# Decode attention of two blocks: V's loads ahead of K's, V's product ahead of K's sums, and another map from rows to partitions

## The chip, the core and the metric

The kernel runs on one core of one Trainium2 chip. The metric is the time of one execution in microseconds (us), as the device measures it. Engines are named as in the profile: PE (matrix engine), DVE (vector engine), ACT (scalar engine), POOL, and SP, which here only issues transfers. The 16 load engines that move data between the chip's main memory and the on-chip memory are called DMA.

## The reference, cut to what matters

Two independent attention blocks A and B, one new token per sequence, each with its own weights and its own cache. The results of the two blocks are put side by side.

```python
# per block: B = 2 sequences, 32 heads, Sk = 8192 tokens, Dh = 192, D = 640, all bfloat16
q = (x @ wq).reshape(B, 1, 32, 192).transpose(0, 2, 1, 3)
scores = einsum("bhqd,bhkd->bhqk", q, k_cache) * 192 ** -0.5
p = softmax(scores)
o = einsum("bhqk,bhkd->bhqd", p, v_cache)
out = o.transpose(0, 2, 1, 3).reshape(B, 1, 32 * 192) @ wo
```

Each K and each V is read once: 2 blocks x 2 sequences x 32 heads x 8192 x 192 x 2 bytes x 2 is 805 MB, nearly all of the 837 MB that are read.

## The kernel before, in words

**Units and thirds.** The work is cut into 16 units of eight heads of one sequence (`UH = 8`, `NU = 16`). A unit's K is 8 x 8192 x 192 numbers; each of the 128 partitions holds a sixteenth of one head, 512 tokens. In before partition p holds head p div 16 and sixteenth p mod 16. K and V of a unit come in three thirds (`NCH = 3`), each a load of 128 rows of `ROW` = 32768 numbers (64 KiB). A third is 170 whole tokens and a fragment. Only three buffers for thirds (`NBUF = 3`) fit on chip; they are taken in turn by the list `loads` (L229 to L233), and SP issues load i when the work that reads load i-3 is done (`done`, L490, and L499 to L501): for a third of K its last sum on PE, `("sl", u, c)`, for a third of V its last product, `("pv", u, c)`.

**K's side.** For a third of K, DVE multiplies the tokens by the unit's q in place, in five pieces (`dve_mul`, names `("m", c, k)`, L303; the fragments go into `pad`, L301). PE sums the 192 products of a token down to 16 with twelve matmuls against the identity (`pe_sum`, `("s", c, k)`, L415) into one of three banks, and DVE reduces these to one score (`dve_red`, `("r", c, k)`, L311). The ten tokens that are left of each third, and the fragments, go through `pe_rest` (`("sl", c)`, L427) and `dve_rest` (`("rl",)`, L315).

**Softmax.** When all scores of a unit are there: the maximum of each partition (`mx`, L319), set out by head with `mask` (`mp`, L322), the maximum over partitions on POOL (`ar`, L339), its negative for each partition (`nm`, `nb`), the exponential on ACT (`exp`, L361), and the spread (`sp`, L334), which writes P into `pb`, eight columns a token of which only the partition's head's is not zero.

**V's side.** PE multiplies P by a third of V, two tokens at a time (`pe_pv`, `("pv", c)`, L445 and L451), after `pe_l` (`("l",)`, L433) has summed the exponentials. When the last third is done DVE takes the reciprocal and the two halves of the result (`rc`, `oh`, `os`, L342 to L348), ACT scales it (`of`, L351), and PE puts the eight rows in place in the result of all heads (`pl`, L457).

**The order.** Each engine has one list of instructions, written out by the loop L564 to L608 with `put(engine, unit, name, function, waits)`. In an engine the order of the `put` calls is the order of execution; between engines it is the semaphores of the named waits. In slot u stands K's work of unit u and V's work of unit u-1 (`lag` -1). In before PE's slot u is: sums of K's first third, `l`, V's first third; sums of K's second third, V's second third; sums of K's last third, q of the next unit, V's last third; `pl`. DVE's slot u is: for each third the five products with the reduction of the piece before behind each, and the last reduction; then `rl`, `mx`, `mp`, `nm`, `nb`; `rc`, `oh`, `os`; `sp`. Slots 1 to 15 are emitted as a loop.

**Other places.** The map from rows to partitions stands in the source of the load (`ld_kv`, L269), in `mask` (which partition has which head, L530), and in `esel`, which spreads q from its projection to the partitions (L523, `dve_su` L293, `pe_q` L403). After the last unit, the result is turned (L466) and multiplied by the output weights (L479), which take the buffers of V's first two thirds.

Of the kernel before, what the change touches and what calls it, by code (L numbers as in the profile page):

```python
# [5 lines left out]
ALU = mybir.AluOpType  # L6
ACTF = mybir.ActivationFunctionType
AXL = mybir.AxisListType
# [111 lines left out]
def build_kernel(nc, blocks, out):  # L120
    NBLK = len(blocks)
    B, Hn, Sk, Dh = blocks[0]["k"].shape
# [33 lines left out]
    with ExitStack() as es:  # L156
# [72 lines left out]
        loads = [("k", 0, c) for c in range(NCH)]  # L229
        for u in range(1, NU):  # L230
            for c in range(NCH):
                loads += [("k", u, c), ("v", u - 1, c)]
        loads += [("v", LASTU, c) for c in range(NCH)]  # L233
        buf = {}
        for i, key in enumerate(loads):
# [16 lines left out]
        def dma(out_ap, in_ap, k):  # L252
            s = reg[k][0]
            return lambda eng: eng.dma_start(out_ap, in_ap).then_inc(s, 16)
# [13 lines left out]

        def ld_kv(kind, u, c):  # L269
            qb, hg = u // HG, u % HG  # L270
            src = blocks[qb // B][kind][qb % B, UH * hg:UH * hg + UH].rearrange("h t d -> (h t d)")
            src = src.rearrange("(p n) -> p n", p=128)
            return dma(bufs[buf[kind, u, c]], src[:, c * ROW:(c + 1) * ROW], (kind, u, c))

        def tokens(b, c, lo, n):
            return bufs[b][:, OFF[c] + lo * Dh:OFF[c] + (lo + n) * Dh].rearrange("p (t d) -> p t d", d=Dh)
# [15 lines left out]
        def dve_su(u):  # L292
            return lambda eng: eng.tensor_tensor(su[:], esel[:], onehot[:, S_dve.at(u)].broadcast_to([128, 144]), ALU.mult)  # L293
# [107 lines left out]
            return fn  # L401

        def pe_q(eng):  # L403
            eng.matmul(outps[:, 0:Dh], su[:, 16:144], qc[:, 0:Dh], start=True, stop=False)
            return eng.matmul(outps[:, 0:Dh], su[:, 0:128], qc[:, Dh:QW], start=False, stop=True)  # L405

        def pe_zero(eng):
# [153 lines left out]
        def put(eng, slot, name, fn, waits, lag=0):  # L561
            slots[eng].setdefault(slot, []).append((name, fn, [w for w in waits if w is not None], lag))

        for u in range(NU + 1):  # L564
            real, old = u < NU, u >= 1
            v = u - 1

            def back(*k):
                return k if k[1] >= -1 else None
            if real:  # L570
                put("dve", u, ("su", 1), dve_su(u + 1), [("q", u)])
                for c in range(NCH):
                    for k in range(NSUB):
                        w = [("k", u, c), ("qe", u), ("sl", u - 1, NCH - 1) if u and c == 0 else None]
                        put("dve", u, ("m", c, k), dve_mul(u, c, k), w)
                        put("pe", u, ("s", c, k), pe_sum(u, c, k), [("m", u, c, k), prev(u, c, k)])
                        if k:
                            put("dve", u, ("r", c, k - 1), dve_red(u, c, k - 1),
                                [("s", u, c, k - 1), ("sp", u - 1) if u else None])
                    put("dve", u, ("r", c, NSUB - 1), dve_red(u, c, NSUB - 1), [("s", u, c, NSUB - 1)])  # L580
                    put("pe", u, ("sl", c), pe_rest(u, c),
                        [("m", u, c, NSUB - 1), ("rl", u - 1) if u and c == 0 else None])
                    if c == NCH - 1:
                        put("dve", u, ("rl",), dve_rest, [("sl", u, c)])
                        put("dve", u, ("mx",), dve_max, [("rl", u)])
                        put("dve", u, ("mp",), dve_mp, [("mx", u), ("ar", u - 1) if u else None, ("negm",)])
                        put("dve", u, ("nm",), dve_nm, [("ar", u)])
                        put("dve", u, ("nb",), dve_nb, [("nm", u), ("exp", u - 1) if u else None])
                        put("pe", u, ("q", 1), pe_q, [("su", u + 1), ("qe", u)])
                        put("pool", u, ("ar",), pool_ar, [("mp", u), ("nm", u - 1) if u else None])  # L590
                        put("act", u, ("qe", 1), act_q, [("q", u + 1), ("m", u, NCH - 1, NSUB - 1)])
                    if old:
                        if c == 0:
                            put("pe", u, ("l", -1), pe_l, [("exp", v), ("sp", v), ("os", v - 1), ("rc", v - 1)])
                        put("pe", u, ("pv", c, -1), pe_pv(v, c), [("v", v, c)])
            else:
                put("pe", u, ("l", -1), pe_l, [("exp", v), ("sp", v), ("os", v - 1), ("rc", v - 1)])
                for c in range(NCH):
                    put("pe", u, ("pv", c, -1), pe_pv(v, c), [("v", v, c)])
            if old:  # L600
# [5 lines left out]
            if real:  # L606
                put("act", u, ("exp",), act_exp, [("nb", u), ("l", v) if u else None])
                put("dve", u, ("sp",), dve_spread, [("exp", u), ("pv", v, NCH - 1) if u else None, ("mask",)])  # L608
# [6 lines left out]
        for e, S in streams.items():  # L615
            order = [n for n, *_ in slots[e][1]]
            have = {n for n, *_ in slots[e][0]}
            after = {}
            at = None
            for n in order:  # L620
                if n in have:
                    at = n
                else:
                    after.setdefault(at, []).append(full(n, 0))
            for u in sorted(slots[e]):
                for n, fn, waits, _ in slots[e][u]:
                    S.add(fn, waits=waits, sig=full(n, u), tag=(u, n),
                          pre=after.get(None, ()) if u == 0 and n == order[0] else (),
                          post=after.get(n, ()) if u == 0 else ())

        S_dve.add(dve_oall(0), waits=[("pl", LASTU), ("q", NU)], sig=("oa", 0))
# [84 lines left out]
```

## Time and profile before

| | us |
|---|---|
| median of 3 runs (lowest, highest) | 1956.53 (1955.77, 1956.9) |
| the profiled execution's own time | 1958.03 |
| its span, first to last instruction | 1956.1 |
| PE busy, DVE busy, ACT busy | 1518.4, 1121.2, 28.4 |
| share of the 16 DMA engines, page's part 3 | 99.0% |

The profile is of one execution, and times in its views count from its first instruction. In a timeline each row is: start, duration, engine, line of the code, operation, what it writes and reads, how many (x), and in brackets the engine's idle time just before it and what ended that. In a table by stretches each engine's busy time stands with its number of instructions, then the granted clock of PE, the share of the DMA engines, and GB/s. Busy times of PE are of pipelined instructions, so a start is a better mark than an end.

### The profile page before, as it was taken

The page shows a single profiled execution, that of the slowest core. Times are in us where ns is not written, and L with a number is a line of the kernel's source. Part 1 is how long each engine was busy: PE and PEld are TensorE (multiplying, and loading weights), DVE is VectorE, ACT ScalarE, POOL GpSimd, SP SyncE. Part 2 cuts the span into 40 slices and gives each one's busy share as a digit, 9 for nine tenths or more (in the row PEclk, how much of TensorE's full clock was granted, in tenths as well). Part 3 has the DMA queues.
Part 4 walks back from the last instruction along what each step waited for, and adds up shares of the span by engine and source line. Part 5 has one row for each costly group of instructions (what it writes and reads, how often), then busy time and mean ns, then how long its engine had stood idle before and what let it go on. Part 6 is the DMA issues. An engine that isn't in the chain of part 4 may idle for free.

```text
span 1956.1 us, 18384 instructions
## 1 busy us (share of the span) xinstructions
PE 1518.4 (78%) x8256; PEld 774.8 (40%) x8256; DVE 1121.2 (57%) x771; ACT 28.4 (1%) x76; POOL 8.9 (0%) x60
## 2 busy tenths in 40 slices
PE   4658868688786968968697886868878686886888
PEld 3224434344343433433343443434434343343354
DVE  0686566555665556466546655655566556646610
ACT  0000000000000000000000000000000000000000
POOL 0000000000000000000000000000000000000000
PEclk9789989899898989989899998989989898998999
DMA  9996999999999999999999999999999999999998
GB/s 428 427 425 287 447 429 429 433 429 429 438 434 434 430 430 436 434 436 430 433 433 437 433 430 433 436 434 434 430 433 440 432 430 433 434 437 433 430 433 383
DMA packets 15149, 836.97 MB, mean 428 GB/s; under 512 B 1688, under 2 KB 1824, under 8 KB 2208
## 3 DMA queue, kind: packets, MB, share of 16 engines
q1 hardware_dynamic: 15136, 836.78, 99.0%
q8 instruction: 10, 0.16, 0.0%
q14 instruction: 3, 0.02, 0.0%
HBM read 836.77 MB, written 0.01 MB: 428 GB/s over the span
## 4 chain that ended last, share of the span: by engine, by line
PE 48%; DVE 31%; DMA 13%; issue 7%; ACT 1%; another core or an unknown queue 0%; DVEq 0%; SPq 0%; ACTq 0%; POOL 0%
PE ops L445 30%; DVE big L303 24%; PE scps L415 15%; DMA big<-in_B_k_cache_dram 9%; DVE sc L311 3%; DVE pb L334 2%; PE rest L427 2%; DMA big<-in_B_wo_dram 2%; DMA big<-in_B_wq_dram 2%; PE scps L397 1%; ACT sc L361 1%; PE ops L451 0%; DVE o_hi L345 0%; DVE o_hi L348 0%
## 5 line engine op out<-in xcount | busy, mean ns | idle before, releaser
L415 PE MATMUL scps<-big,ident 128*128 128x512 bf16 x2880 | 737.2, 413 | 374.9 <-DVE big L303 374.6
L303 DVE TENSOR_TENSOR big<-big,qt 128x6144 bf16<-128x6144 bf16 (+1 forms) x240 | 847.8, 3549 | 0.0
L445 PE MATMUL ops<-big,pb 128*40 128x384 bf16 x4080 | 682.0, 327 | 2.4 <-DMA big<-in_B_v_cache_dram 2.4
L415 PEld LDWEIGHTS scps<-big,ident 128*128 128x128 bf16 x2880 | 285.0, 105 | 815.9 <-DVE big L303 455.2
L445 PEld LDWEIGHTS ops<-big,pb 128*40 128x40 bf16 x4080 | 404.5, 100 | 258.1 <-issue 4.3
L311 DVE TENSOR_REDUCE sc<-scps 128x32 f32<-128x512 f32 x240 | 164.6, 686 | 274.1 <-PE scps L415 273.9
L301 DVE TENSOR_TENSOR pad<-big,qt 128x128 bf16<-128x128 bf16 (+1 forms) x64 | 11.8, 205 | 228.1 <-DMA big<-in_B_k_cache_dram 130.2
L342 DVE RECIPROCAL rc<-ops 8x1 f32<-8x1 f32 x16 | 2.5, 156 | 223.8 <-PE ops L445 223.8
L334 DVE TENSOR_TENSOR pb<-sc,mask 128x2048 bf16<-128x2048 f32 x32 | 71.9, 2288 | 19.3 <-ACT sc L361 19.3
L427 PE MATMUL rest<-big,ident 128*128 128x160 bf16 x576 | 48.1, 234 | 0.0
L427 PEld LDWEIGHTS rest<-big,ident 128*128 128x128 bf16 x576 | 43.0, 98 | 11.7 <-issue 0.6
L397 PE MATMUL scps<-big,pb 128*64 128x384 bf16 x160 | 27.7, 336 | 3.2 <-DMA big<-in_B_wq_dram 2.6
L354 ACT ACTIVATE qt<-outps 128x192 bf16<-128x192 f32 x17 | 5.6, 331 | 1579.4 <-PE outps L405 1579.4
L457 PE MATMUL oall<-o_sb,place 8*128 8x192 bf16 x16 | 4.0, 249 | 25.3 <-ACT o_sb L351 25.3
L397 PEld LDWEIGHTS scps<-big,pb 128*64 128x64 bf16 x160 | 18.1, 114 | 12.5 <-DMA big<-in_B_wq_dram 3.0
L293 DVE TENSOR_TENSOR su<-esel,onehot 128x144 bf16<-128x144 bf16 x17 | 5.1, 301 | 28.5 <-PE outps L405 28.5
L389 PE MATMUL rest<-ident,pb 4*128 4x4 bf16 x5 | 0.4, 178 | 21.5 <-DMA pb<-in_B_x_dram 21.5
L315 DVE TENSOR_REDUCE sc<-rest 128x30 f32<-128x480 f32 x16 | 10.5, 658 | 6.9 <-PE rest L427 6.9
L339 POOL PARTITION_ALL_REDUCE mg<-mp x16 | 5.9, 367 | 1855.6 <-DVE mp L322 1855.6
L457 PEld LDWEIGHTS oall<-o_sb,place 8*128 (+1 forms) x16 | 1.4, 90 | 31.4 <-issue 29.5
L290 DVE CAST pb<-rest 128x5 bf16<-128x5 f32 x4 | 0.4, 171 | 19.2 <-PE rest L389 19.2
L361 ACT ACTIVATE sc<-sc,nb 128x512 f32<-128x512 f32 x16 | 11.3, 706 | 2.1 <-DVE nb L328 2.1
(66 smaller groups left out, 131.3 us busy)
## 6 DMA issues: line engine op xcount, KB each, us to landing
big<-in_B_wq_dram SPq DMA_DIRECT2D x1, 7680.0 KB, 37.2
big<-in_A_wo_dram SPq DMA_DIRECT2D x1, 7680.0 KB, 35.0
big<-in_A_wq_dram SPq DMA_DIRECT2D x1, 7168.0 KB, 20.1
big<-in_B_wo_dram SPq DMA_DIRECT2D x1, 4640.0 KB, 32.0
big<-in_B_wo_dram SPq DMA_DIRECT2D x1, 1760.0 KB, 35.8
big<-in_B_wo_dram SPq DMA_DIRECT2D x1, 800.0 KB, 37.3
big<-in_A_wq_dram SPq DMA_DIRECT2D x1, 512.0 KB, 3.6
big<-in_A_k_cache_dram SPq DMA_DIRECT2D x24, 33.7
```

What stands on the lines that cost most here:

```text
L301: eng.tensor_tensor(pad[:, t, lo:hi], src, qt[:, 0, lo:hi], ALU.mult)
L303: return eng.tensor_tensor(t, t, qt[:].broadcast_to([128, size(k), Dh]), ALU.mult)
L311: return lambda eng: eng.tensor_reduce(sc[:, lo:lo + SUB], scps[bank(u, c, k)][:], AXL.X, ALU.add)
L315: eng.tensor_reduce(dst, rest[:, 0:NCH * REST, :].rearrange("p (c t) g -> p c t g", c=NCH), AXL.X, ALU.add)
L334: ins = eng.tensor_tensor(dst[:, :, a], src[:, :, a].unsqueeze(3).broadcast_to([128, TP // 8, 4, UH]), mask[:].unsqueeze(1).unsqueeze(1).b ...
L339: return eng.partition_all_reduce(mg[:], mp[:], 128, bass.bass_isa.ReduceOp.max)
L354: return eng.activation(qt[:, 0, :], outps[:, 0:Dh], ACTF.Identity)
L361: return eng.activation(sc[:], sc[:], ACTF.Exp, bias=nb[:], scale=scale, accum_out=rs[:])
L397: ins = eng.matmul(flat[blk][64 * blk:64 * blk + 64, 0:QW], xz[:, blk, c, XM - m:XM - m + 64], wq_t[blk][:, c, QW * m:QW * m + QW], start= ...
L415: ins = eng.matmul(scps[bank(u, c, k)][:], ident[:], t[:, :, j * DG:(j + 1) * DG], start=(j == 0), stop=(j == NJ - 1))
L427: ins = eng.matmul(rest[:, lo:lo + n, :], ident[:], src[:, :, j * DG:(j + 1) * DG], start=(j == 0), stop=(j == NJ - 1))
L445: ins = eng.matmul(ops[0:MP, 0:QW], pb[:, j0:j0 + MP], bufs[b][:, OFF[c] + j * QW:OFF[c] + (j + 1) * QW], start=(c == 0 and j == 0), stop= ...
```

## The change

The list of loads puts each third of V ahead of the third of K that it was behind. The source of a K or V load is read as 16 sixteenths of 8 heads, so that partition p holds head p mod 8 and sixteenth p div 8; `mask`, `esel` and the column of `pe_q` follow.

On the engines, in slot u from 1 on, V's product of a third now stands ahead of the sums of K's third on PE, `l` ahead of the first. The three DVE steps behind V's last product, and ACT's scaling, stand ahead of the products of K's last third; `pl` stands behind the first sum of that third. The last reduction of a third stands behind the first product of the next third (in unit 0 too). The softmax stands at the end of the slot, and behind it comes the next slot, with V's first product, which reads its P.

```diff
         for u in range(1, NU):
             for c in range(NCH):
-                loads += [("k", u, c), ("v", u - 1, c)]
+                loads += [("v", u - 1, c), ("k", u, c)]
...
         def ld_kv(kind, u, c):
             qb, hg = u // HG, u % HG
-            src = blocks[qb // B][kind][qb % B, UH * hg:UH * hg + UH].rearrange("h t d -> (h t d)")
-            src = src.rearrange("(p n) -> p n", p=128)
-            return dma(bufs[buf[kind, u, c]], src[:, c * ROW:(c + 1) * ROW], (kind, u, c))
+            src = blocks[qb // B][kind][qb % B, UH * hg:UH * hg + UH].rearrange("h t d -> h (t d)")
+            src = src.rearrange("h (i n) -> i h n", n=NCH * ROW)[:, :, c * ROW:(c + 1) * ROW]
+            return dma(bufs[buf[kind, u, c]], src, (kind, u, c))
...
-            eng.matmul(outps[:, 0:Dh], su[:, 16:144], qc[:, 0:Dh], start=True, stop=False)
+            eng.matmul(outps[:, 0:Dh], su[:, 1:129], qc[:, 0:Dh], start=True, stop=False)
...
-        S_dve.add(lambda eng: eng.tensor_copy(esel[:, 16:144].rearrange("p (t y) -> p t y", t=GP)[:, :, 0:16],
-                                              em[:].unsqueeze(2).broadcast_to([128, GP, 16])),
+        S_dve.add(lambda eng: eng.tensor_copy(esel[:, 1:129].rearrange("p (i t e) -> p i t e", t=GP, e=2)[:, :, :, 0],
+                                              em[:].unsqueeze(1).broadcast_to([128, 16, GP])),
...
-        S_dve.add(lambda eng: eng.tensor_reduce(mask[:], ident[:].rearrange("p (h y) -> p h y", y=16), AXL.X, ALU.add),
+        S_dve.add(lambda eng: eng.tensor_reduce(mask[:], ident[:].rearrange("p (i h) -> p h i", h=UH), AXL.X, ALU.add),
...
+            def red(c, k):
+                put("dve", u, ("r", c, k), dve_red(u, c, k), [("s", u, c, k), ("sp", u - 1) if u else None])
+
+            def turn_out():
                 put("dve", u, ("rc", -1), dve_rc, [("pv", v, NCH - 1), ("of", v - 1)])
                 put("dve", u, ("oh", -1), dve_ohi, [("of", v - 1)])
                 put("dve", u, ("os", -1), dve_osum, [("oh", v)])
                 put("act", u, ("of", -1), act_of, [("os", v), ("rc", v), ("pl", v - 1)])
+
+            def v_part(c):
+                if c == 0:
+                    put("pe", u, ("l", -1), pe_l, [("exp", v), ("sp", v), ("os", v - 1), ("rc", v - 1)])
+                put("pe", u, ("pv", c, -1), pe_pv(v, c), [("v", v, c)])
...
+            put("dve", u, ("su", 1), dve_su(u + 1), [("q", u)])
+            for c in range(NCH):
+                if old:
+                    v_part(c)
+                if old and c == NCH - 1:
+                    turn_out()
+                for k in range(NSUB):
+                    w = [("k", u, c), ("qe", u), ("sl", u - 1, NCH - 1) if u and c == 0 else None]
+                    put("dve", u, ("m", c, k), dve_mul(u, c, k), w)
+                    put("pe", u, ("s", c, k), pe_sum(u, c, k), [("m", u, c, k), prev(u, c, k)])
+                    if old and c == NCH - 1 and k == 0:
+                        put("pe", u, ("pl", -1), pe_pl(v), [("of", v)])
+                    if k:
+                        red(c, k - 1)
+                    elif c:
+                        red(c - 1, NSUB - 1)
+                put("pe", u, ("sl", c), pe_rest(u, c),
+                    [("m", u, c, NSUB - 1), ("rl", u - 1) if u and c == 0 else None])
+            c = NCH - 1
+            red(c, NSUB - 1)
+            put("dve", u, ("rl",), dve_rest, [("sl", u, c)])
+            put("dve", u, ("mx",), dve_max, [("rl", u)])
+            put("dve", u, ("mp",), dve_mp, [("mx", u), ("ar", u - 1) if u else None, ("negm",)])
+            put("dve", u, ("nm",), dve_nm, [("ar", u)])
+            put("dve", u, ("nb",), dve_nb, [("nm", u), ("exp", u - 1) if u else None])
+            put("pe", u, ("q", 1), pe_q, [("su", u + 1), ("qe", u)])
+            put("pool", u, ("ar",), pool_ar, [("mp", u), ("nm", u - 1) if u else None])
+            put("act", u, ("qe", 1), act_q, [("q", u + 1), ("m", u, NCH - 1, NSUB - 1)])
+            put("act", u, ("exp",), act_exp, [("nb", u), ("l", v) if u else None])
+            put("dve", u, ("sp",), dve_spread, [("exp", u), ("pv", v, NCH - 1) if u else None, ("mask",)])
```

More of the change, by code (lines that the diff above doesn't have):

```diff
@@ L566, in build_kernel @@
             v = u - 1
[L568 to L599, printed above, removed]
@@ L600, in build_kernel @@
-            if old:
+            def red(c, k):
+                put("dve", u, ("r", c, k), dve_red(u, c, k), [("s", u, c, k), ("sp", u - 1) if u else None])
+            def turn_out():
                 put("dve", u, ("rc", -1), dve_rc, [("pv", v, NCH - 1), ("of", v - 1)])
@@ L604, in build_kernel @@
                 put("act", u, ("of", -1), act_of, [("os", v), ("rc", v), ("pl", v - 1)])
-                put("pe", u, ("pl", -1), pe_pl(v), [("of", v)])
-            if real:
-                put("act", u, ("exp",), act_exp, [("nb", u), ("l", v) if u else None])
-                put("dve", u, ("sp",), dve_spread, [("exp", u), ("pv", v, NCH - 1) if u else None, ("mask",)])
+            def v_part(c):
+                if c == 0:
+                    put("pe", u, ("l", -1), pe_l, [("exp", v), ("sp", v), ("os", v - 1), ("rc", v - 1)])
+                put("pe", u, ("pv", c, -1), pe_pv(v, c), [("v", v, c)])
@@ new lines, in build_kernel @@
+            if not real:
+                for c in range(NCH):
+                    v_part(c)
+                turn_out()
+                put("pe", u, ("pl", -1), pe_pl(v), [("of", v)])
+                continue
+            put("dve", u, ("su", 1), dve_su(u + 1), [("q", u)])
+            for c in range(NCH):
+                if old:
+                    v_part(c)
+                if old and c == NCH - 1:
+                    turn_out()
+                for k in range(NSUB):
[10 more added lines that the diff above has]
+                    [("m", u, c, NSUB - 1), ("rl", u - 1) if u and c == 0 else None])
@@ L627, in build_kernel @@
                     S.add(fn, waits=waits, sig=full(n, u), tag=(u, n),
-                          pre=after.get(None, ()) if u == 0 and n == order[0] else (),
+                          pre=after.get(None, ()) if u == 0 and n == slots[e][0][0][0] else (),
                           post=after.get(n, ()) if u == 0 else ())
```

## The prediction

> **What bounds the kernel now.** I read first the page's slices (share of the load engines and what they moved), then busy time by stretches, then the issues of the loads, then the timeline of TensorE (PE) and VectorE (DVE) over one unit of the steady stretch.
>
> ```profile
> span 1956.1 us, 18384 instructions
> DMA  9996999999999999999999999999999999999998
> GB/s 428 427 425 287 447 429 429 433 429 429 438 434 434 430 430 436 434 436 430 433 433 437 433 430 433 436 434 434 430 433 440 432 430 433 434 437 433 430 433 383
> ```
>
> ```profile
> 60.20:156.90 96.70, 59.95 (x259) 25.25 (x260) 80.49 (x50) 1.15 (x3) 0.37 (x1) 0.83 0.99 423
> 156.90:170.90 14.00, 10.80 (x52) 4.64 (x50) 10.05 (x8) 0.00 (x0) 0.00 (x0) 0.88 0.00 1
> 170.90:1900.00 1729.10, 1372.01 (x7389) 699.63 (x7387) 1024.08 (x676) 22.34 (x60) 5.51 (x15) 0.93 1.00 433
> ```
>
> The load engines are full (share 1.00, last but one column; GB/s in the last) except in one hole of 14.0 us. A load is 128 rows of 64 KiB, 8.389 MB; six of them, one unit (eight heads, their K and V), take 50.33 / 433 = 116.2 us. So loads look like the only bound. The issues say more:
>
> ```profile
> 135.18 0.33 SPq L254 DMA_DIRECT2D big<-in_A_k_cache_dram  x1
> 169.96 0.33 SPq L254 DMA_DIRECT2D big<-in_A_v_cache_dram  x1
> ...
> 866.67 0.33 SPq L254 DMA_DIRECT2D big<-in_A_v_cache_dram  x1
> ...
> 982.73 0.33 SPq L254 DMA_DIRECT2D big<-in_A_v_cache_dram  x1
> 997.03 0.33 SPq L254 DMA_DIRECT2D big<-in_B_k_cache_dram  x1
> ```
>
> The rows at 866.67 and 982.73 are the same issue (the second third of V, released by the first third of K) one unit apart: 116.06 us. Between them the engines' own chain has no slack either:
>
> ```profile
> 880.88 5.35 PE L415 MATMUL scps<-big,ident 128*128 128x512 bf16 x24
> ...
> 896.42 2.76 PE L415 MATMUL scps<-big,ident 128*128 128x512 bf16 x12 [2.10 <-DVE big L303]
> ...
> 899.94 0.34 PE L445 MATMUL ops<-big,pb 128*40 128x384 bf16 x1
> ...
> 914.13 5.45 PE L415 MATMUL scps<-big,ident 128*128 128x512 bf16 x24
> ...
> 929.67 4.42 PE L415 MATMUL scps<-big,ident 128*128 128x512 bf16 x12 [2.10 <-DVE big L303]
> ...
> 935.31 0.34 PE L445 MATMUL ops<-big,pb 128*40 128x384 bf16 x1
> ...
> 959.91 7.24 PE L415 MATMUL scps<-big,ident 128*128 128x512 bf16 x24 [8.52 <-DVE big L303]
> ...
> 982.63 0.19 PE L433 MATMUL ops<-rs,mask 128*8 128x1 f32 x2
> ```
>
> ```profile
> 935.25 0.66 DVE L315 TENSOR_REDUCE sc<-rest 128x30 f32<-128x480 f32 x1 [0.43 <-PE rest L427]
> ...
> 949.60 0.16 DVE L342 RECIPROCAL rc<-ops 8x1 f32<-8x1 f32 x1 [11.75 <-PE ops L445]
> 949.78 0.35 DVE L345 COPY o_hi<-ops 8x192 f32<-8x192 f32 x1
> 950.17 0.34 DVE L348 TENSOR_TENSOR o_hi<-ops,o_hi 8x192 f32<-8x192 f32 x1
> 951.74 4.49 DVE L334 TENSOR_TENSOR pb<-sc,mask 128x2048 bf16<-128x2048 f32 x2 [1.23 <-ACT sc L361]
> ...
> 956.37 0.22 DVE L301 TENSOR_TENSOR pad<-big,qt 128x128 bf16<-128x128 bf16 x1
> ```
>
> PE's work of a third of K (five sums and the rest) and of a third of V follow each other, each starting where the last ended: V 899.94 to 914.13 (14.2), K 914.13 to 935.31 (21.2), V 935.31 to 949.60 (14.3), a break to 959.91 (10.3), K 959.91 to 982.63 (22.7), V 982.63 to 997.03 (14.4), and K once more as from 880.88 to 899.94 (19.1). The sum is 116.2, within rounding of the period: the chain has the loads' pace by its own length, and has no slack to give. A third of K differs by the clock: the last sum takes 2.76 at full clock and 4.42 when it meets a slow stretch. Those come at the same place in each unit, in pieces of about 3.4 us or three of them:
>
> ```profile
> 953.60:963.70 10.10, 3.79 (x9) 1.35 (x10) 9.52 (x6) 0.00 (x0) 0.00 (x0) 0.50 1.00 435
> 977.50:980.80 3.30, 3.30 (x8) 1.14 (x9) 0.49 (x1) 0.00 (x0) 0.00 (x0) 0.50 0.92 397
> 1069.60:1079.70 10.10, 3.73 (x9) 1.35 (x10) 9.58 (x6) 0.00 (x0) 0.00 (x0) 0.50 1.00 435
> 1093.50:1096.90 3.40, 3.40 (x9) 1.20 (x10) 0.54 (x1) 0.00 (x0) 0.00 (x0) 0.50 0.89 386
> ```
>
> The granted clock (third column from the end) is 0.50 throughout these, and full around them.
>
> **The change, part by part.** *The loads' order.* In before the fourth load is the next K, which lies unread while the softmax of unit 0 runs, and V's second third (issued 169.96) waits until that K is summed: that is the hole. With V ahead, V's first third takes the place, and the next free buffer comes from its product with P, which can start right behind the softmax, 14.2 us of PE work, instead of behind a whole third of K. The hole goes: 14.0 us for the loads, worth that much where loads set the end, and nothing where the chain does.
>
> *Unit 0's sums.* The last reduction of a third now stands behind the first product of the next, so DVE no longer waits for it. PE's idle time ahead of the first sum of the second and of the last third goes:
>
> ```profile
> 90.18 6.91 PE L415 MATMUL scps<-big,ident 128*128 128x512 bf16 x24 [3.06 <-DVE big L303]
> ...
> 114.23 6.84 PE L415 MATMUL scps<-big,ident 128*128 128x512 bf16 x24 [3.35 <-DVE big L303]
> ```
>
> That is 6.4 us. Those thirds of K have landed by then, since their products start right behind the reduction.
>
> *The order on PE and DVE from unit 1 on* is the large part, and it is where I part from the loads. Before, a unit's last V product stands behind the last third of K, and covers the row maximum, its spread over partitions and the bias; only from the reciprocal to the first sum is PE idle: 949.60 to 959.91, 10.3 us. After, PE's next work behind the last third of K is the V product of *that* unit's P, which waits for the whole softmax. Its length stands bare in unit 0, from the reduction of the rest to the end of the spread:
>
> ```profile
> 135.18 0.66 DVE L315 TENSOR_REDUCE sc<-rest 128x30 f32<-128x480 f32 x1 [0.43 <-PE rest L427]
> ...
> 138.73 4.49 DVE L334 TENSOR_TENSOR pb<-sc,mask 128x2048 bf16<-128x2048 f32 x2 [0.88 <-ACT sc L361]
> ```
>
> 138.73 + 4.49 - 135.18 = 8.0 us, and 0.15 from there to the first matmul of l (below), where before had 935.31 - 935.25 = 0.1. A second break arises ahead of the last third of K: the reciprocal and the two copies (949.60 to 950.5, 0.9) now stand on DVE ahead of its first product and wait for the last V product, and the product itself is bare, 956.37 to 959.91, 3.5. DVE queues behind that reciprocal all products of the third; PE's sums wait for them. Breaks: 8.1 + 0.9 + 3.5 = 12.5 in place of 10.3, so 2.2 longer. The first products of the other two thirds are covered by V products of 14.2.
>
> Two breaks also mean two slow restarts. Before, one third of K starts after a break (22.7 against 19.1). After, the last third does, and the first V product too. That product after a break is in the tail of before:
>
> ```profile
> 1883.97 0.19 PE L433 MATMUL ops<-rs,mask 128*8 128x1 f32 x2 [4.98 <-DVE pb L334]
> ...
> 1900.56 0.33 SPq L254 DMA_DIRECT2D big<-in_A_wo_dram  x1
> ...
> 1914.63 2.23 SPq L254 DMA_DIRECT2D big<-in_B_wo_dram  x5
> ...
> 1931.32 0.15 DVE L342 RECIPROCAL rc<-ops 8x1 f32<-8x1 f32 x1 [47.50 <-PE ops L445]
> ```
>
> 16.6 from 1883.97 to its end, against 14.2 to 14.4: 2.3 more. So the chain of a unit is 116.1 + 2.2 + 2.3 = 120.6 with one of the two remaining thirds meeting a slow stretch as now, 4.42 - 2.76 = 1.7 less with none, 118.9, and 1.7 more with both, 122.3. Before's stretches keep their place from unit to unit, so the chain settles on a length that brings it back to the same place; among 118.9, 120.6 and 122.3 I take 119.5, one 3.4 us stretch above now. [...]
>
> *The rows.* A load still has the same 128 rows of 64 KiB at the same addresses; only which row goes to which partition changes. At 433 GB/s in every long stretch I take no gain and no loss; the chain now leaves the loads 119.5 - 116.2 = 3.3 us a unit to spare. The set-up of mask, esel and su has as many instructions as before and runs under the first weight loads; weights for q read from an odd column, if slower, lie in the 8 us in which PE idles; uncovered, some tenths a unit.
>
> *The sum.* Unit 0's spread ends at 143.2 - 6.4 = 136.8. Fifteen units of 119.5 bring the last one to 1929.3. From there, by the rows of the tail: 0.15, 16.6, 14.1, 14.3 bring the last reciprocal to 1974.5. From it to the end of the span before took 1956.1 - 1931.3 = 24.8, with waits for the output weights in it:
>
> ```profile
> 1935.65 8.36 PE L479 MATMUL outps<-big,oT 128*2 128x320 bf16 x96 [1.50 <-DMA big<-in_A_wo_dram]
> ...
> 1946.66 5.88 PE L479 MATMUL scps<-big,oT 128*2 128x320 bf16 x80 [0.81 <-DMA big<-in_B_wo_dram]
> ```
>
> After, these are issued some 29 and 15 us ahead of the last reciprocal and land in some 21 and 18 more, just in time; about 2 us go, 22.6 are left: a span of 1997. Against the same row of before (1931.3) that is 43 later. The profiled execution's own time is 1958.03, 1.9 above its span and 1.5 above the median of the runs, 1956.5; so a span of 1997 is a median of 1997.4, and I write 1997.
>
> **The rivals.** *The chain keeps the loads' pace.* If it came out at 116.2 or less, the loads would run full from end to end: by the sum above 1997 - 15 x (119.5 - 116.2) = 1948, and by the loads alone 1956.5 - 14.0 = 1942.5, so 1948. It needs both other thirds at full clock and no slow restart of the V product: 118.9 - 2.3 = 116.6, nearly that. For it: 0.4 is little. Against: every break of 8 us or more on PE in these rows is followed by slow clock. It decides below a chain of 116.8, where 15 x 2.7 = 40.5 less gives the time of before, *no change*.
>
> *The chain settles one stretch higher,* at 122.3 with both thirds slow: 15 x 2.8 = 42 more, 2039. For it: in before two of three thirds of K already meet slow clock. Against: here all three must.
>
> *The loads become slower by the new rows.* It decides from 119.5 / 6 = 19.9 us a load, 421 GB/s. The lowest mean of a long stretch above is 423 (60.2 to 156.9), six loads in 119.0: no effect. The far end is the one load of short rows:
>
> ```profile
> big<-in_A_wq_dram SPq DMA_DIRECT2D x1, 512.0 KB, 3.6
> ```
>
> 0.524 MB in 3.6 us, 146 GB/s, issue and landing included: 345 us a unit and some 5400 in all. The new loads keep their long rows and are nearest to the first, so I price the rival at a tenth under 433: 390, 21.5 us a load, 129 a unit, 1997 + 15 x 9.5 = 2140. [...]
>
> **How the numbers follow.** The forecast gets 0.61, with its own range 1982 to 2015 (chain 118.5 to 120.7); loads' pace at 1948: 0.17; no change by cancellation: 0.03; one stretch higher: 0.11; slower loads: 0.08. The range takes in the first three and the lower part of the fourth: 1942 to 2030. A measurement of this kernel tells 0.2%, 4 us, from no change. Faster is the second case and 0.01 of the forecast's tail, 0.18; same 0.03; slower 0.79.
>
> **What would show it.** The hole near 157 to 171 is gone, and the load engines' share from 250 us on falls from 1.00 to about 116.2 / 119.5 = 0.97, 421 GB/s. The same issue one unit apart is 119.5 us later, not 116.1. PE idles some 8 us ahead of each l, released by DVE's spread, and some 4.4 us ahead of the last third's first sum. I am wrong if DVE still waits for K's landing at the steady pace with the share at 1.00 (first rival), or if single loads take over 19.9 us (last).

## The result, and the profile after

The changed kernel takes 3924.28 us, median of four runs (3908.88 to 3955.93), against 1956.72 us for the kernel before, timed beside it on the same chip (1955.77 to 1957.37, four runs): a ratio of 2.0077, 95% interval 1.9938 to 2.0216. The forecast was 1997, in a range of 1942 to 2030. The profiled execution has a span of 3934.1 us and took 3936.74.

| | before | after |
|---|---|---|
| span of the profiled execution, us | 1956.1 | 3934.1 |
| packets, and MB moved | 15149, 836.97 | 15148, 836.96 |
| share and GB/s in the steady stretch | 1.00, 433 | 1.00, 210 |
| one load of K or V, us | 19.4 | 40.2 |

First the page of the changed kernel: the span, then the share of the load engines and what they moved in 40 slices, then what was moved in all and through which queue.

```profile
span 3934.1 us, 18441 instructions
...
DMA  9999999999999999999999999999999999999998
GB/s 288 213 205 212 208 208 213 211 207 211 211 207 211 213 209 207 213 211 209 209 213 211 207 211 211 208 211 212 210 207 213 208 209 210 209 209 210 207 211 250
DMA packets 15148, 836.96 MB, mean 213 GB/s; under 512 B 1688, under 2 KB 1824, under 8 KB 2208
...
q1 hardware_dynamic: 15136, 836.78, 99.8%
```

The engines are as full as before and have no hole. They move the same bytes in the same number of packets (15136 in the loads' queue, before and after), so no row was cut into pieces; they only move them at half the rate, 210 GB/s against 433. The trace's record of packets says the same row by row: a K or V row of 64 KiB takes 5.07 us in the median and 4.47 at the least, where the kernel before has 2.42 in the median. The first slice, at 288, holds the loads of wq, which the change leaves alone. Next, loads as they were issued in the same kernel: SyncE's (SP's) timeline, in which the second row is six issues behind the first, and then the first load of wq with its median us from issue to landing.

```profile
1021.42 0.54 SPq L254 DMA_DIRECT2D big<-in_A_k_cache_dram  x1
...
1262.88 0.54 SPq L254 DMA_DIRECT2D big<-in_A_k_cache_dram  x1
```

```profile
big<-in_A_wq_dram SPq DMA_DIRECT2D x1, 7168.0 KB, 20.2
```

One unit of six loads takes 241.5 us, 40.2 a load, where 8.389 MB at 433 GB/s take 19.4. The 7.3 MB of wq land in 20.2 us in the same execution, so it is not the chip or the queue that is slow, but these loads. That explains the whole time: there are 96 of them, and the prediction's time by the loads alone, 1942.5, with 96 x (40.2 - 19.4) more is 3939, against 3936.74.

What the engines now wait for, by the view of waits of the changed kernel (us in total, times, longest):

```profile
DVE pad L301 <- DMA big<-in_B_k_cache_dram: 1011.4, 24, 58.9
DVE pad L301 <- DMA big<-in_A_k_cache_dram: 951.2, 24, 58.7
...
PE ops L445 <- DMA big<-in_B_v_cache_dram: 295.8, 24, 27.3
...
PE ops L445 <- DMA big<-in_A_v_cache_dram: 265.6, 24, 15.9
```

VectorE waits for the landing of every one of the 48 thirds of K, 1962.6 us in all, and TensorE for every third of V, 561.4. The kernel before, in the same view:

```profile
DVE pad L301 <- DMA big<-in_B_k_cache_dram: 130.2, 16, 11.6
DVE pad L301 <- DMA big<-in_A_k_cache_dram: 97.9, 14, 10.1
...
PE ops L445 <- DMA big<-in_B_v_cache_dram: 2.4, 1, 2.4
```

There it was 228.1 us for K, and for V next to nothing. The chain of the engines, on which the forecast rested, is now hidden behind the loads altogether.

### The profile page after: what moved, and what is told of

It is laid out like the page before. It is cut to its first block, busy times and chain, and to the rows that moved or that the text cites. A ratio compares the mean times of both kernels' runs of the same rounds, so it can differ in the third digit from the quotient of the medians.

```text
span 3934.1 us, 18441 instructions
## 1 busy us (share of the span) xinstructions
PE 1704.7 (43%) x8256; PEld 828.6 (21%) x8256; DVE 1120.2 (28%) x771; ACT 30.1 (1%) x76; POOL 8.9 (0%) x60
## 2 busy tenths in 40 slices
DMA packets 15148, 836.96 MB, mean 213 GB/s; under 512 B 1688, under 2 KB 1824, under 8 KB 2208
## 3 DMA queue, kind: packets, MB, share of 16 engines
q1 hardware_dynamic: 15136, 836.78, 99.8%
## 4 chain that ended last, share of the span: by engine, by line
another core or an unknown queue 53%; DVE 17%; PE 17%; issue 11%; DMA 1%; POOL 0%; ACT 0%; DVEq 0%; SPq 0%; ACTq 0%; POOLq 0%
DVE big L303 13%; PE scps L415 9%; PE ops L445 7%; DVE sc L311 2%; DMA big<-in_B_wq_dram 1%; DVE pb L334 1%; PE rest L427 1%; PE scps L397 0%; DVE rmax L319 0%; PE outps L479 0%; PE scps L479 0%; POOL mg L339 0%; DVE o_hi L345 0%; DVE o_hi L348 0%
## 5 line engine op out<-in xcount | busy, mean ns | idle before, releaser
L415 PE MATMUL scps<-big,ident 128*128 128x512 bf16 x2880 | 816.6, 446 | 1511.4 <-DVE big L303 1511.4
L445 PE MATMUL ops<-big,pb 128*40 128x384 bf16 x4080 | 779.4, 357 | 561.4 <-DMA big<-in_B_v_cache_dram 295.8
L415 PEld LDWEIGHTS scps<-big,ident 128*128 128x128 bf16 x2880 | 302.5, 111 | 2006.4 <-DVE big L303 1600.3
L445 PEld LDWEIGHTS ops<-big,pb 128*40 128x40 bf16 x4080 | 437.5, 108 | 879.4 <-DMA big<-in_B_v_cache_dram 300.2
L301 DVE TENSOR_TENSOR pad<-big,qt 128x128 bf16<-128x128 bf16 (+1 forms) x64 | 11.9, 207 | 1962.6 <-DMA big<-in_B_k_cache_dram 1011.4
L451 PE MATMUL ops<-big,pb 128*8 128x128 bf16 (+1 forms) x64 | 12.9, 248 | 0.0
## 6 DMA issues: line engine op xcount, KB each, us to landing
big<-in_A_wq_dram SPq DMA_DIRECT2D x1, 7168.0 KB, 20.2
```

The source lines that it names most:

```text
L301: eng.tensor_tensor(pad[:, t, lo:hi], src, qt[:, 0, lo:hi], ALU.mult)
L415: ins = eng.matmul(scps[bank(u, c, k)][:], ident[:], t[:, :, j * DG:(j + 1) * DG], start=(j == 0), stop=(j == NJ - 1))
L445: ins = eng.matmul(ops[0:MP, 0:QW], pb[:, j0:j0 + MP], bufs[b][:, OFF[c] + j * QW:OFF[c] + (j + 1) * QW], start=(c == 0 and j == 0), stop= ...
L451: eng.matmul(ops[0:UH, lo:hi], pb[:, j0:j0 + UH], src, start=False, stop=False, skip_group_check=True)
```

## The experiments

Two questions were open. Is the forecast of the order (a chain of 119.5 us a unit) right where the rows don't hide it? And what makes the new rows slow? For the second there were two theories. **A**: the shape of the source decides, 16 groups of 8 rows in place of 128 even rows, however far apart they lie. **B**: the distance of neighbouring rows decides, 3 MiB in place of 192 KiB. A was later split: **A1**, the shape decides which partitions are written at one time, and the rate goes by those; **A2**, three levels are slow as such. **A3** is that transfers of 64 rows are slow as such. A kernel that a theory holds to be slow was expected at the changed kernel's 40 us a load, some 3900 us in all, and one that it holds to be as fast as before at 19.4 and 1957. For A1 the author assumed that 64 neighbouring partitions from 0 or from 64 on are slow together and that 32 to 95 are not.

The order alone and the rows alone came first. Where one time is given below, the kernel ran once, which is enough to tell 1960 us from 3900.

**The changed kernel with the rows of before.** Order and reductions stay as changed; the partition of each row, mask, esel and the query's weights are those of before.

```diff
-src = blocks[qb // B][kind][qb % B, UH * hg:UH * hg + UH].rearrange("h t d -> h (t d)")
-src = src.rearrange("h (i n) -> i h n", n=NCH * ROW)[:, :, c * ROW:(c + 1) * ROW]
-return dma(bufs[buf[kind, u, c]], src, (kind, u, c))
+src = blocks[qb // B][kind][qb % B, UH * hg:UH * hg + UH].rearrange("h t d -> (h t d)")
+src = src.rearrange("(p n) -> p n", p=128)
+return dma(bufs[buf[kind, u, c]], src[:, c * ROW:(c + 1) * ROW], (kind, u, c))
...
```

> The changed kernel with the rows of before: partition p holds head p div 16 and sixteenth p mod 16, the load's source has two levels again; the order of loads and of the engines stays the changed one. Both theories of the loads (the new source shape, the new distance between neighbouring rows) expect loads of 19.4 us again and a time near 2000. What it tells apart is the order: my chain of 119.5 us a unit gives 1997 with the DMA share at 0.97; the rival, a chain at the loads' pace of 116.1, gives 1942 to 1948 with the share at 1.00.

It took 1995.33 us (1995.10 to 1996.53, four runs), a ratio to before of 1.0203, 95% interval 1.0186 to 1.0220. Busy time by stretches (granted clock, share and GB/s in the last three columns):

```profile
250.00:1900.00 1650.00, 1290.95 (x6806) 652.59 (x6807) 955.10 (x632) 22.05 (x55) 4.75 (x13) 0.93 0.98 422
156.90:170.90 14.00, 9.24 (x36) 3.41 (x34) 11.51 (x6) 0.00 (x0) 0.00 (x0) 0.89 1.04 449
```

SP's timeline of this kernel, the same load one unit apart:

```profile
869.87 0.33 SPq L254 DMA_DIRECT2D big<-in_A_k_cache_dram  x1
...
989.35 0.33 SPq L254 DMA_DIRECT2D big<-in_B_k_cache_dram  x1
```

The hole at 156.9 to 170.9 is gone, the load engines have slack (0.98), and a unit takes 119.48. So the order costs 2%, and what is left of the doubling lies with the rows, which the next kernel has alone.

**The new rows alone**, in the order of before: the reverse edit on the kernel before.

> The kernel before with the new rows alone; the order of loads and engines is that of before. If the rows alone make the loads slow, a load takes 40.1 us as in the changed kernel and the time is 3900 to 3950. If the order has a part in it (V's and K's loads side by side in another sequence), a load is faster than 40 and the time falls clearly under 3900.

It took 3920.16 us. The steady stretch:

```profile
250.00:3800.00 3550.00, 1532.74 (x7330) 744.45 (x7328) 1026.86 (x678) 22.32 (x60) 5.48 (x15) 0.72 1.00 212
```

212 GB/s at a share of 1.00, as in the changed kernel. The rows do it by themselves, and the order makes no difference beside them that these runs could show (3920.16 against 3908.88 to 3955.93).

**The shape with near rows.** Before, with loads of 16 groups of 8 rows where all rows of a group lie 192 KiB apart as before, and the groups nine of those apart.

```diff
+src = blocks[qb // B][kind].rearrange("b h t d -> (b h t d)").rearrange("(r n) -> r n", n=NCH * ROW)
+r = min(128 * (HG * (qb % B) + hg), 1024 - 144)
+src = src[r:r + 144].rearrange("(a b) n -> a b n", b=9)[:, 0:8, c * ROW:(c + 1) * ROW]
+return dma(bufs[buf[kind, u, c]], src, (kind, u, c))
```

> The kernel before, whose loads read other rows: 16 groups of 8 rows, the rows of a group 192 KiB apart as in before, the groups 9 x 192 KiB apart, so that the source can't be folded into two levels (16 is its slowest level). It reads the wrong rows of K and V, as many bytes in rows of the same length, so the output isn't the reference's. [...] Theory B (neighbouring rows 3 MiB apart are slow to read): 19.4 us a load, 1957.

**The distance with the shape of before.** Before, with 128 even rows 1.5 MiB apart.

```diff
+src = blocks[qb // B][kind].rearrange("b h t d -> (b h t d)").rearrange("(p n) -> p n", p=128)
+j = NCH * (HG * (qb % B) + hg) + c
+return dma(bufs[buf[kind, u, c]], src[:, j * ROW:(j + 1) * ROW], (kind, u, c))
```

> The kernel before, whose loads read 128 rows 1.5 MiB apart, a two-level source over all heads of both sequences. It reads the wrong rows of K and V, as many bytes in rows of the same length, so the output isn't the reference's. Theory A (shape of the source): 19.4 us a load, 1957. Theory B (distance of neighbouring rows): clearly slower than 19.4, towards 40, a time of 2300 to 3900.

Near rows in 16 groups took 3930.47 us, and far rows in one level 1958.18. Their steady stretches, in this order:

```profile
250.00:3800.00 3550.00, 1516.26 (x7274) 737.21 (x7271) 1026.88 (x678) 22.32 (x60) 5.48 (x15) 0.72 1.00 211
```

```profile
250.00:1900.00 1650.00, 1305.55 (x6990) 662.73 (x6989) 981.78 (x649) 22.02 (x59) 5.14 (x14) 0.93 1.00 433
```

The distance falls as a cause: eight times before's distance costs nothing, and before's own distance in 16 groups costs everything. Of the two, the shape decides. The next three kernels ask what in it. All three are before with the loads changed.

**A load in two transfers**, partitions 0 to 63 and then 64 to 127, each in two levels:

```diff
-reg[key] = (bsem[i % NBUF], 16 * (i // NBUF + 1))
+reg[key] = (bsem[i % NBUF], 32 * (i // NBUF + 1))
...
+dst = bufs[buf[kind, u, c]]
...
+dma(dst[0:64], src[0:64], (kind, u, c))(eng)
+return dma(dst[64:128], src[64:128], (kind, u, c))(eng)
```

> The kernel before, each K or V load cut in two transfers, partitions 0 to 63 and then 64 to 127; rows, addresses and the two-level source as before. [...] Theory A2 (a source of three levels is slow by itself, whatever partitions the engines write): 19.4 us a load, 1957.

**A load in three transfers**, 32 to 95 first:

```diff
+reg[key] = (bsem[i % NBUF], 48 * (i // NBUF + 1))
...
+for lo, hi in ((32, 96), (0, 32), (96, 128)):
+    ins = dma(dst[lo:hi], src[lo:hi], (kind, u, c))(eng)
```

> The kernel before, each load cut in three transfers, partitions 32 to 95, then 0 to 31, then 96 to 127; rows and addresses as before. [...] Theory A2, or transfers that cost by their number: 19.4 to 20 a load, 1957 to 2010. [...]

**Three levels with the slowest at 128**: each partition gets two pieces of 32 KiB that lie 96 KiB apart.

```diff
+src = src.rearrange("(p x n) -> p x n", p=128, x=2)[:, :, c * (ROW // 2):(c + 1) * (ROW // 2)]
+return dma(bufs[buf[kind, u, c]].rearrange("p (x n) -> p x n", x=2), src, (kind, u, c))
```

> The kernel before with a three-level source whose slowest level is 128: each partition's row is read in two pieces of 32 KiB, 96 KiB apart. It reads other bytes of K and V, as many of them, so the output isn't the reference's. [...] Theory A2 (three levels are slow): 40 us a load, 3900.

The two halves took 3958.64 us, the three transfers 3796.1 and the three levels of 128 took 1963.12. The steady stretch of the halves, the page's slices of the three transfers, and the steady stretch of the three levels:

```profile
250.00:3800.00 3550.00, 1779.38 (x7237) 804.63 (x7236) 1021.66 (x673) 21.16 (x57) 5.48 (x15) 0.62 1.00 208
```

```profile
GB/s 342 249 225 197 205 230 220 235 240 205 190 207 228 238 236 223 221 208 207 228 227 231 233 215 206 210 212 216 211 213 210 211 220 211 211 218 212 210 217 197
```

```profile
250.00:1900.00 1650.00, 1292.73 (x6953) 657.33 (x6952) 981.10 (x649) 21.99 (x59) 5.12 (x14) 0.93 1.00 431
```

A2 falls: three levels run at 431 GB/s, as A1 expected of these. The halves, with two plain levels each, are as slow as 16 groups (208 GB/s against 211). That fits A1 and A3 alike. The three transfers were to tell those apart, and by their time they did not: under A1 I expected about 2885 (9.7 us for half a load at full rate and 19.4 for the other half at half rate, 29 us a load, an estimate from the 19.4 and 40.2 us above), and the time is only 4% under that of the halves. The second slice, the first without loads of wq, stands at 249 GB/s, where the changed kernel has 213, and the later ones swing between 190 and 240 and settle near 211. Their first load tells more. Its 128 rows in two stretches, the 64 rows of partitions 32 to 95 and then the other 64, and a long stretch of the second half beside them:

```profile
38.50:48.20 9.70, 8.74 (x54) 5.99 (x55) 0.00 (x0) 0.00 (x0) 0.00 (x0) 1.00 1.03 434
48.20:67.80 19.60, 4.97 (x31) 2.98 (x29) 0.31 (x1) 0.81 (x2) 0.00 (x0) 0.69 1.00 211
1900.00:3700.00 1800.00, 807.36 (x3827) 391.31 (x3825) 522.72 (x348) 11.90 (x32) 2.92 (x8) 0.73 1.00 215
```

The first load takes 29.3 us, as A1 had it: 64 rows at 434 GB/s (2.42 us a row in the median) and 64 at 211 (5.03). That speaks against A3, since the first of these transfers has 64 rows and is not slow. After that the fast rows die out: in the second half of the run 4 of 6144 rows take less than 2.6 us. The forecast of 2885 took every load to be like the first. So that each rate stands by itself, the next two kernels take the mixture out.

**Only 64 partitions loaded.** Before, where all loads but those of unit 0's K bring only partitions 32 to 95, or only 0 to 63 (in the second kernel).

```diff
+p = slice(0, 128) if kind == "k" and u == 0 else slice(32, 96)
+return dma(bufs[buf[kind, u, c]][p], src[p], (kind, u, c))
```

> The kernel before, whose loads from the first V on bring only the rows of partitions 32 to 95 (half the data; the other half keeps what lies there, so the output isn't the reference's). One transfer of 64 rows a load. [...] Rival A3 (transfers of 64 rows are slow whatever their partitions): 22 us. [...]

> The same with the rows of partitions 0 to 63 alone: as many rows, bytes and transfers as with 32 to 95. [...] Rival A3: the same figure as with 32 to 95, whichever that is. The time is the chain's, 1920 to 1960.

They took 1952.31 and 2050.61 us, a little above the 1920 to 1950 expected for the first and well above the 1920 to 1960 for the second. For a load that finds the queue empty A1 expected 12 us from issue to landing in the first and 22 in the second, estimates from rows of 2.4 and 5 us, and A3 the same in both. Partitions 32 to 95: queue total, median us from issue to landing, and a steady stretch:

```profile
q1 hardware_dynamic: 9184, 446.71, 55.6%
...
big<-in_A_k_cache_dram SPq DMA_DIRECT2D x24, 12.3
```

```profile
1100.00:1900.00 800.00, 638.94 (x3448) 327.19 (x3447) 464.76 (x308) 10.42 (x28) 2.56 (x7) 0.93 0.54 220
```

Partitions 0 to 63, the same three rows:

```profile
q1 hardware_dynamic: 9184, 446.71, 99.3%
...
big<-in_A_k_cache_dram SPq DMA_DIRECT2D x24, 40.2
```

```profile
1100.00:1900.00 800.00, 613.50 (x3210) 308.30 (x3209) 457.44 (x301) 10.09 (x27) 2.19 (x6) 0.91 1.00 206
```

The same number of rows, packets and bytes: the middle 64 partitions need little over half of the time that the engines have (220 GB/s at a share of 0.54, so 407 while they run), and the first 64 need all of it, at 206 GB/s; their 40.2 is mostly waiting in the queue, and 4.194 MB at 206 are 20.4 us a load, against 12.3 from issue to landing. A row takes 2.42 us in the median in the first kernel and 5.12 in the second. Six loads of 20.4 us are 122.4, longer than the engines' 116, which the expected 1920 to 1960 had left out. Both kernels read 64 neighbouring rows at the same distances, so the reading side doesn't tell them apart. A3 falls, and for one transfer of 64 rows A1 holds: **it is which partitions are written together that sets the rate**, 206 GB/s for 0 to 63 and 407 for 32 to 95. Why the two sets differ isn't shown.

**How fine must the groups be?** The shape with near rows again, in 32 groups of 4 rows and in 64 groups of 2. Are these slow like 16 groups of 8, some 3900 us, or as fast as before, 1957?

```diff
-r = min(128 * (HG * (qb % B) + hg), 1024 - 144)
-src = src[r:r + 144].rearrange("(a b) n -> a b n", b=9)[:, 0:8, c * ROW:(c + 1) * ROW]
+r = min(128 * (HG * (qb % B) + hg), 1024 - 160)
+src = src[r:r + 160].rearrange("(a b) n -> a b n", b=5)[:, 0:4, c * ROW:(c + 1) * ROW]
```

```diff
+r = min(128 * (HG * (qb % B) + hg), 1024 - 192)
+src = src[r:r + 192].rearrange("(a b) n -> a b n", b=3)[:, 0:2, c * ROW:(c + 1) * ROW]
```

> The kernel before, whose loads read 32 groups of 4 neighbouring rows, the groups 5 x 192 KiB apart: a three-level source with 32 as its slowest level. It reads wrong rows of K and V, as many bytes, so the output isn't the reference's. [...]

> The same with 64 groups of 2 rows, 3 x 192 KiB apart. [...]

1961.05 and 1956.05 us, with steady stretches:

```profile
250.00:1900.00 1650.00, 1298.08 (x6994) 661.39 (x6992) 981.22 (x649) 22.01 (x59) 5.13 (x14) 0.93 1.00 433
```

```profile
250.00:1900.00 1650.00, 1293.59 (x6988) 659.78 (x6989) 980.87 (x649) 22.00 (x59) 5.12 (x14) 0.94 1.00 433
```

Both run at full rate, 433 GB/s. Of the shapes tried for one transfer to 128 partitions, 16 groups of 8 alone is slow (210 to 212 GB/s), though it writes all 128, the fast 32 to 95 among them. That this shape is slow by the partitions that are written at one time, as A1 has it, was the author's inference from the rates and isn't shown: which engine writes which partition isn't in the records. A cause on the reading side has no run of its own there; the two sources of this shape read groups 192 KiB and 9 x 192 KiB apart, and run alike (210 and 211 GB/s).

**The first third of V ahead, and nothing else.** The last kernel takes from the change only what acts in units 0 and 1: before's rows, before's order from unit 2 on, unit 0's reductions as changed, and one third of V ahead of K in unit 1. Slot 1 is therefore written out, and the loop starts at slot 2.

```diff
-loads += [("k", u, c), ("v", u - 1, c)]
+loads += [("v", 0, 0), ("k", 1, 0)] if (u, c) == (1, 0) else [("k", u, c), ("v", u - 1, c)]
...
+if u == 1 and c == 0:
+    put("pe", u, ("l", -1), pe_l, [("exp", v), ("sp", v), ("os", v - 1), ("rc", v - 1)])
+    put("pe", u, ("pv", c, -1), pe_pv(v, c), [("v", v, c)])
...
+elif c and not u:
+    put("dve", u, ("r", c - 1, NSUB - 1), dve_red(u, c - 1, NSUB - 1), [("s", u, c - 1, NSUB - 1)])
...
```

> The kernel before with two things of the changed order in units 0 and 1 alone: the last reduction of a third behind the first product of the next one in unit 0, and the first third of V ahead of the first third of K in loads and on PE in unit 1. From unit 2 on as before, with before's rows. By my chain theory the unit keeps 116.1, unit 0 is 6.4 shorter and the hole of 14 us in the loads goes: loads full from end to end, 1942, share 1.00. By its rival (a steady chain sets the end, and the hole counts for nothing) 1950, 6.4 less; by the rival that V ahead costs in unit 1 what unit 0 gains: 1955.

It took 1950.09 us (1948.68 to 1951.05, six runs): a ratio to before of 0.9963, 95% interval 0.9949 to 0.9976, so it is faster than before by 0.4%, and the only one of the orders tried that is. By stretches:

```profile
156.90:170.90 14.00, 9.12 (x48) 4.16 (x48) 11.74 (x10) 0.00 (x0) 0.00 (x0) 1.00 1.02 440
170.90:290.00 119.10, 93.25 (x472) 46.31 (x473) 74.81 (x48) 1.49 (x4) 0.37 (x1) 0.89 0.93 397
290.00:1900.00 1610.00, 1273.29 (x6880) 650.11 (x6879) 948.17 (x628) 20.84 (x56) 5.12 (x14) 0.94 1.00 433
```

The hole of 14.0 us is closed, but only 6.2 us come out of it (1956.27, the median of before beside it, less 1950.09), about the 6.4 of unit 0's sums; part of the hole comes back as a share of 0.93 in the next 119 us. This is the rival's 1950, and not the 1942 that I expected for a gain of the whole hole: the engines' chain sets the end, and the loads don't.

## Why the prediction was right or wrong, point by point

**The rows: wrong, and this is the step that failed.** "A load still has the same 128 rows of 64 KiB at the same addresses; only which row goes to which partition changes. At 433 GB/s in every long stretch I take no gain and no loss." The first half is true: bytes and packets are unchanged. The error is to take the rate of 433 GB/s as a property of rows and bytes. It goes with the shape of the load as well (16 groups of 8 rows ran at 210 to 212) and with the partitions written (0 to 63 ran at 206), and the change's new map from rows to partitions brought that shape: 40.2 us a load in place of 19.4. The row of wq that I priced by, 512 KB in 3.6 us, and all loads of before had even rows for their 128 partitions, so no row of before bore on a source of 16 groups. The far end of 5400 was named and then set aside; without a row of that shape the cost was unknown, and a chance of 0.08 was too small for it.

**The rival of slower loads: the right case, at the wrong price.** Its point of decision, 19.9 us a load, was passed by a factor of two. It was priced at 21.5 us a load and 2140 us, "nearest to the first" of two ends because the rows stay long; the time lies between 2140 and the far end of 5400. Distance isn't where the price lay: rows 1.5 MiB apart ran at 433 GB/s, and rows 192 KiB apart in 16 groups at 211. At these distances, with rows of 64 KiB, no run here shows a loss by distance; none has 128 even rows at 2 MiB or 3 MiB.

**The order on PE and DVE: right.** With the rows of before, the forecast of 1997 became 1995.33, and the chain of 119.5 a unit 119.48. Its terms, in the timelines of that kernel (PE, then DVE; start, us, and in brackets the idle time before and its releaser):

```profile
885.42 2.76 PE L415 MATMUL scps<-big,ident 128*128 128x512 bf16 x12 [2.10 <-DVE big L303]
...
918.67 4.45 PE L415 MATMUL scps<-big,ident 128*128 128x512 bf16 x12 [2.10 <-DVE big L303]
...
942.54 4.45 PE L415 MATMUL scps<-big,ident 128*128 128x512 bf16 x12 [4.41 <-DVE big L303]
...
973.41 0.20 PE L433 MATMUL ops<-rs,mask 128*8 128x1 f32 x2 [7.89 <-DVE pb L334]
...
989.25 5.35 PE L415 MATMUL scps<-big,ident 128*128 128x512 bf16 x24
```

```profile
131.10 4.49 DVE L334 TENSOR_TENSOR pb<-sc,mask 128x2048 bf16<-128x2048 f32 x2 [0.88 <-ACT sc L361]
...
938.17 0.16 DVE L342 RECIPROCAL rc<-ops 8x1 f32<-8x1 f32 x1 [18.95 <-PE ops L445]
...
965.38 0.66 DVE L315 TENSOR_REDUCE sc<-rest 128x30 f32<-128x480 f32 x1 [0.43 <-PE rest L427]
...
968.86 4.49 DVE L334 TENSOR_TENSOR pb<-sc,mask 128x2048 bf16<-128x2048 f32 x2 [0.88 <-ACT sc L361]
```

- The bare softmax, 8.0 us: from 965.38 to 968.86 + 4.49 it is 8.0, and PE is idle 7.89 ahead of l. It recurs in every unit, which the waits of this kernel show in one row:

```profile
PE ops L433 <- DVE pb L334: 126.4, 16, 8.0
```

- The break ahead of the last third, 0.9 + 3.5 = 4.4: PE is idle 4.41, and the reciprocal that DVE stands behind is 4.37 ahead of the first sum.
- The second slow restart: the product behind l runs from 973.41 to 989.25, 15.8 where I had 16.6 from the tail. This term was 0.8 too long.
- One of the other two thirds meeting slow clock: of their last sums one takes 2.76 and one 4.45, as taken for the length of 120.6; with the shorter restart that is 119.8, and the breaks are 12.3, not 12.5. So the terms alone give 119.6, beside 119.48. The settling that the prediction argued for can be seen all the same: from one unit to the next this kernel's length falls 120.15, 119.87, 119.68, 119.57 and then stays at 119.46 to 119.52, and before's falls from 116.30 to 116.05 and stays at 116.05 to 116.09 but for one of 115.55 (each the same issue of a V load, one unit apart). The two end 3.4 us apart, the length of one slow stretch. That it is the clock's stretches that hold it there has no run of its own, so no run shows the 119.5 as the length that such stretches set; what was measured in its place is 119.48.
- Unit 0's spread ends at 131.10 + 4.49 = 135.6; I had 136.8. The hole is gone, as said.

The share I named for the steady stretch was 0.97 at 421 GB/s; it is 0.98 at 422.

**The rivals on the order.** Those of the loads' pace (1948) and of a stretch higher (2039) fall with that run, at 1995.33. In the changed kernel neither could show, since the loads hide the chain.

**The base of the sum: right, by three runs.** The plainest is the kernel that loads only partitions 32 to 95. Its load engines are idle for almost half of the time, and VectorE waits for the landing of K once; SP's timeline has the same issue one unit apart:

```profile
866.60 0.51 SPq L254 DMA_DIRECT2D big<-in_A_v_cache_dram  x1
...
982.66 0.51 SPq L254 DMA_DIRECT2D big<-in_A_v_cache_dram  x1
```

```profile
DVE pad L302 <- DMA big<-in_A_k_cache_dram: 4.9, 1, 4.9
```

A unit still takes 116.06 us, to the hundredth what it takes before, and the time is 1952.31, about 3 us under that of before beside it (1955.28). So the length of the chain is the engines' own, and full load engines bound almost nothing of it. That is why an order that gives the loads work without a hole gained nothing, and why the last kernel gains 6.2 and not 14.0.

## What to carry to other kernels

When an edit changes which row of a load goes to which partition, the rate must be taken as unknown, even with the same bytes, addresses and packets: look at the shape of the source and time one such load before building on it. In these runs a slowest level of 32, 64 or 128 kept the full rate (431 to 433 GB/s), and one of 16 halved it (210 to 212). An even busy share says nothing on this (1.00 at 433 and at 210 here); look at GB/s beside it. And where loads are full and a serial chain of engines has their pace as well, removing a hole from the loads pays only what the chain gives up too (6.2 us of a hole of 14.0 here). Loading half of the bytes and looking whether the unit gets shorter tells which of the two sets the pace.

## What the runs showed of the hardware

- Written partitions set the rate of a transfer of 64 rows: 64 partitions, 0 to 63, move at 206 GB/s, 5.12 us a row of 64 KiB, and 32 to 95 at about 407 with the same bytes, 2.42 us a row.
- Of one transfer to 128 partitions, 16 groups of 8 rows run at 210 to 212 GB/s, and 32 by 4, 64 by 2 and 128 with two pieces each at 431 to 433. Half of 433 would be 216.5; why 16 groups run 2 to 3% under that, and partitions 0 to 63 5%, isn't known.
- Three transfers of 64, 32 and 32 partitions start with a load at 434 and then 211 GB/s, 29.3 us, and come down to 215 GB/s over the second half of the run. The fast rows die out (4 of 6144 there take less than 2.6 us), and nothing here tests why.
- SP's issue takes 0.33 us for 128 even rows (433 GB/s), 0.54 for the three levels of the new rows (210 GB/s), and 0.51 for the 64 even rows of partitions 32 to 95 (about 407). The length of the issue doesn't go with the rate, and with the load engines' share at 1.00 it lies off the path.
- A cure that keeps the new rows was not tried: none of the full-rate shapes above puts eight heads on neighbouring partitions.
